# Padding the last keys of v, copying a product in its own tile, and one clamp on another engine: a fused attention and feed-forward kernel

## The chip, the cores and the metric

The kernel runs on one core of one Trainium2 chip. Its five engines each have their own queue and run in order: TensorE (PE in the profile, its weight loads are PEld), VectorE (DVE), ScalarE (ACT), GpSimd (POOL) and SyncE (SP, which only issues DMAs). The metric is the device time of one execution in microseconds, and the comparison is with the kernel before on the same chip.

## The reference

Attention over 8 batches, 8 heads, 576 tokens and 64 elements per head, in which a score that lies more than tau below its row's maximum is dropped, followed by two matmuls with a Mish between them:

```python
scores = scale * np.matmul(q, k.transpose(0, 1, 3, 2))
thresh = np.max(scores, axis=-1, keepdims=True) - tau
scores = np.where(scores >= thresh, scores, -1000000000.0)
attn = np.exp(scores - np.max(scores, axis=-1, keepdims=True))
attn = attn / (np.sum(attn, axis=-1, keepdims=True) + 1e-09)
attn_out = np.matmul(attn, v)                 # 8 x 8 x 576 x 64
x = attn_out.transpose(0, 2, 1, 3).reshape(4608, 512)
h = x @ w_in                                  # 512 -> 2048
sp = np.where(h > 20.0, h, np.log1p(np.exp(np.minimum(h, 20.0))))
out = (h * np.tanh(sp)) @ w_out               # 2048 -> 512
```

w_in and w_out reach the kernel as 64-bit floating-point numbers, which it has to turn into pairs of 32-bit parts itself.

## The kernel before

The work comes in **pairs** of heads: 8 batches with 4 pairs each, 32 pairs. Each pair is cut into 9 **tiles** of 128 query rows (8 tiles of one head each, alternating, and a ninth that holds the last 64 rows of both), 288 tiles in all, g = 0 to 287. A loop over g is software-pipelined. In the step for g it issues, in this order:

1. `begin(g + 1)`: the scores of the next tile on PE, into one of two PSUM tiles `s`. A tile `s` is free again when the masking (`masked`, on DVE) two tiles earlier has read it.
2. `product(g - lag)`, which puts the products of a finished half pair into the list `pieces`. It does so twice in a pair, for the first 256 query columns (r = 0, at g % 9 == 7) and for the other 320 (r = 1, at g % 9 == 3). The result y lies in one of **two** PSUM banks of the pool `psh`, which it shares with the results h of the first matmul of the feed-forward part.
3. `evacuate` of tile g - 3: ACT copies the transposed probabilities from PSUM into the tiles `hi` (first head) and `lo` (second head), 128 keys of each of 4 chunks in the partitions, and `tk`, which holds the last 64 keys of the first head in partitions 0 to 63 and those of the second head in partitions 64 to 127.
4. the entries of `pieces`: at g below SOON = 38 two a step, from then on all five, that is 5 chunks for each of two heads on PE.
5. row maximum (DVE), exponential (ACT), the reciprocal (DVE) and normalising (POOL) of the tile before.
6. the **gather** of a finished product: ACT copies y from PSUM to x. The gathers wait in the list `ready`, which is taken over into `done` before the pieces of a step are issued, so that a gather is issued in the step after its product. The gather of r = 1 also closes the pair: `split_x` puts the rounding of x (`xh` on ACT, `xl` on POOL) into `chores`, for the first half of the columns in the same step and for the second half two steps later.
7. `chores`: the rounding of the q and k parts of a later pair (a cast on ACT, a subtraction on POOL), at fixed steps of the 9.
8. `masked` of this tile on DVE, and a number of matmuls of the first feed-forward product (`h<-xh,w1h` and so on): `EVEN = (14, 14, 14, 0, 13, 14, 14, 0, 13)` of them at g % 9 = 0, 1, ..., so none in the two steps with a product, from g = 42 on.
9. the transposes of tile g - 2 on PE (`tp<-ident,p`, `t<-ident,p`).

Every engine executes its instructions in the order in which this loop writes them.

The weights w_in are decoded meanwhile by 32 jobs of 128 x 256 (the class `Decode`, from g = 0 on, the last ones past g = 42): `first` on ACT, then `clamp` in one step, `shift` and `join` in the next on DVE, `add` on POOL, then the upper part on ACT and the lower part on POOL or, for nine of them, on DVE. Before `clamp` in a step stands the normalising of the tile before; behind it stand the chores.

In the product a chunk of 128 keys is a matmul with 128 rows and 64 columns of weights (`vf[:, a, c]`), and the head a decides which half of the partitions of y it writes. The last 64 keys (c = 4) are a matmul with 64 rows and 64 columns for each head: `vf[rows, a, 4]` against `tail[rows, 0, :n]`, where rows are 0 to 63 for the first and 64 to 127 for the second head. In the profile these are the groups `y<-hi,vf`, `y<-lo,vf` and `y<-tk,vf`. After the attention loop come the last feed-forward products, the decoding of w_out and the second matmul (from 960 us on), which the change does not touch.

The methods and functions that the change touches:

Of the kernel before, what the change touches and what calls it, by code (L numbers as in the profile page):

```python
# [9 lines left out]
ALU = mybir.AluOpType  # L10
# [4 lines left out]
P = 128  # L15
B, H, S, D = 8, 8, 576, 64
NP = H // 2
# [11 lines left out]
VP = 32  # L29
SOON = 9 * FULL + 2  # L30
# [47 lines left out]
TOP_MAX = 122879.9921875 * 2.0**-112  # L78


def fv(ap):
    return ap.bitcast(F32)
# [36 lines left out]
class Decode:  # L119
# [16 lines left out]
        nc.scalar.activation(c, low, AF.Copy, scale=2.0**-29)  # L136

    def clamp(self):
        self.nc.vector.tensor_scalar(fv(self.b), fv(self.a), TOP_MAX, -TOP_MAX, ALU.min, ALU.max)

    def shift(self):
        self.nc.vector.tensor_scalar(self.a, self.b, 3, 0x7FFFFFF8, ALU.logical_shift_left, ALU.bitwise_and)
# [18 lines left out]
def attention_moe(tc, q, k, v, tau, w_in, w_out, out):  # L161
    nc = tc.nc
    from contextlib import ExitStack

    with ExitStack() as outer:
# [104 lines left out]
        nc = Engines(tc)  # L270
        with ExitStack() as first:
# [6 lines left out]
            with ExitStack() as att:  # L278
# [160 lines left out]
                def transposes(g):  # L439

                    both = tiles[g]["both"]
                    at = odd(g) * (S + D)
                    tp = pst.tile([P, 4, P], F32, name="tp")
                    for c in range(4):
                        nc.tensor.transpose(tp[:, c, :], both[:, at + c * P:at + (c + 1) * P], ident)
                    t5 = None
                    last = g < 9 * VP and g % 9 == 8
                    if odd(g) or last:
                        t5 = pst.tile([P, P], F32, name="t5")
                        if last:  # L450
                            nc.tensor.transpose(t5, both[:, S - P:S], ident)
                            nc.tensor.transpose(t5[:D], both[:, S - D:S], ident)
                        else:
                            nc.tensor.transpose(t5, both[:, 4 * P:5 * P], ident)
                    return tp, t5
# [51 lines left out]
                def values_full(r, pt, vf, x):  # L507
                    main, tail = pt[r][:2], pt.pop(r)[2]
                    n = (2 + r) * P - r * D
                    y = psh.tile([P, 512], F32, name="y", tag="ph")  # L510

                    def chunk(c):
                        for a in range(2):
                            rows = slice(a * D, (a + 1) * D)
                            if c < 4:
                                w, m = vf[:, a, c], main[a][:, c, :n]
                            else:
                                w, m = vf[rows, a, 4], tail[rows, 0, :n]
                            nc.tensor.matmul(y[rows, :n], w, m, start=c == 0, stop=c == 4)

                    def gather():
                        nc.scalar.copy(x[:, r * QT:r * QT + n], y[:, :n])

                    return [lambda c=c: chunk(c) for c in range(5)], gather
# [118 lines left out]
                ready = []  # L643
# [45 lines left out]
                for g in range(NT + 5):  # L689
# [15 lines left out]
                            tail_hi(g - 3)  # L705
                    if ahead:
                        tiles[g - 2]["tp"] = transposes(g - 2)
                    done = list(ready)
                    ready.clear()
                    for _ in range(5 if g >= SOON else PIECES):  # L710
                        if pieces:
                            work, then = pieces.pop(0)
                            work()
                            if then:
                                ready.append(then)
                    if g < NT:
                        tiles[g]["st"], tiles[g]["e"] = row_max(tiles[g]["s"])
                    if 1 <= g <= NT:
# [160 lines left out]
        for n in range(NG):  # L879
            c, j = divmod(n, NJ)  # L880
# [11 lines left out]
            if c == 0:  # L892
# [5 lines left out]
                for e, d in order:  # L898
                    cols = slice(2 * e * QT + d * P, 2 * e * QT + (d + 1) * P)
                    toks = slice(2 * e * QT, 2 * (e + 1) * QT)  # L900
                    for i, (x, y) in enumerate(((wh, gh), (wh, gl), (wlo, gh))):
                        nc.tensor.matmul(
                            banks[d], x[:, cols], y[:, toks],
                            start=j == e == i == 0, stop=j == NJ - 1 and e == 1 and i == 2,
# [11 lines left out]
            for k, (wi, gi) in enumerate(PRODUCTS):  # L916
                o = banks[k].rearrange("p (n t) -> p n t", t=QT)
                w, at = (wa[j], (0, 2, 3)[wi]) if wi < 3 else (ws[j], wi - 3)
                for b in range(2):
                    cols = slice(at * QT + b * P, at * QT + (b + 1) * P)  # L920
                    for i, (x, y) in enumerate(((0, 0), (0, 1), (1, 0))):
                        nc.tensor.matmul(
                            o[:, b], w[x][:, cols], gs[n][y][:, gi],
                            start=j == b == i == 0, stop=j == NJ - 1 and b == 1 and i == 2,
# [6 lines left out]
def _layout(q, k, v, tau, moe_w_in, moe_w_out):  # L931
    import numpy as np

    f = np.float32
    qt = np.asarray(q, f).reshape(B, NP, 2, S, D).transpose(0, 1, 2, 4, 3)
    qp = np.zeros((B, NP, 2, D, 1280), f)
    qp[:, :, :, :, 0:S] = qt[:, :, 0, None]
    qp[:, :, :, :, 704:768] = qt[:, :, 1, None, :, 512:]
    qp[:, :, :, :, 768:1280] = qt[:, :, 1, None, :, :512]
    kt = np.asarray(k, f).reshape(B, NP, 2, S, D).transpose(0, 1, 4, 2, 3)  # L940
    kp = np.empty((B, NP, 2, D, 2, S + D), f)
    kp[..., :D] = kt[:, :, None, :, :, S - D:]
    kp[..., D:] = kt[:, :, None]
    vt = np.asarray(v, f).reshape(B, NP, 2, S, D)
    vp = np.empty((B, NP, P, 2, 5, D), f)
    vp[:, :, :, :, :4] = vt[:, :, :, :512].reshape(B, NP, 2, 4, P, D).transpose(0, 1, 4, 2, 3, 5)
    for a in range(2):
        vp[:, :, a * D:(a + 1) * D, :, 4] = vt[:, :, :, 512:].transpose(0, 1, 3, 2, 4)
    return {
        "q": qp.reshape(B * NP, P, 1280),  # L950
        "k": kp.reshape(B * NP, P, 2, S + D),
        "v": vp.reshape(B * NP, P, 2, 5, D),
        "tau": np.full((P, 1), tau, f),
        "w_in": np.ascontiguousarray(moe_w_in).view(np.int64),
        "w_out": np.ascontiguousarray(moe_w_out).view(np.int64),
    }
# [18 lines left out]
```

## Time and profile before

| | |
|---|---|
| median of 3 runs | 1377.79 us (1375.15 to 1378.16) |
| profiled execution, whole | 1377.15 us |
| its span, first to last instruction | 1375.4 us |
| PE busy | 1318.8 us, 96% of the span |
| DVE / ACT / POOL busy | 878.1 / 848.0 / 736.9 us |
| first matmul of the feed-forward part | 130.6 us |
| last product of the attention | 949.7 us |

A row of the timeline gives the start (us), the duration (us), the engine, the source line, the operation, its output and inputs, their shapes, how many instructions were merged into the row, and in brackets the idle time of the engine before it with what ended it. All work goes through a helper, so that its line is L95. A row of a group gives the count, then the busy time (us) and the mean of one (ns), then the idle time just before them. A PE matmul's duration reaches over the start of the next one; where it is the pace that matters, starts are to be compared.

### The profile page before, as it was taken

The numbers are of one execution on the slowest core, as the hardware profiler recorded it, in microseconds if no ns is written. First come the engines' busy times: TensorE is split into PE (matmuls) and PEld (weight loads), VectorE is DVE, ScalarE is ACT, GpSimd is POOL, SyncE is SP. The second block draws the span as 40 slices with busy tenths as digits, with TensorE's granted clock in tenths as the row PEclk, the third lists the DMA queues.
The fourth block names the chain that finished last, engine by engine and source line by source line (L and its number), as shares of the span: only waits on it lengthen the run. The fifth ranks groups of instructions, "written<-read, shape, count | busy, mean of one in ns | idle before, by whom it ended". The sixth has DMA issues, their size and how long they took to land. (4 is left out here: it accounts for less than half of the span.)

```text
span 1375.4 us, 28492 instructions
## 1 busy us (share of the span) xinstructions
PE 1318.8 (96%) x9941; PEld 1164.4 (85%) x9941; DVE 878.1 (64%) x2404; ACT 848.0 (62%) x1676; POOL 736.9 (54%) x1061
## 2 busy tenths in 40 slices
PE   8888999999999999999999999999999999999998
PEld 5445888888888888888888888887978999999998
DVE  6998855555555555555555555553997666666664
ACT  4777766666666666666666666664565465555552
POOL 3789866666566656566656566642413334443331
PEclk9889999999999999999999999999999999999999
DMA  5334543323333333333333333311854444444440
GB/s 173 101 101 121 167 123 111 102 85 104 88 95 108 102 88 101 88 98 105 102 91 98 88 100 103 93 43 45 267 165 152 128 124 133 138 136 129 139 135 32
DMA packets 151904, 154.82 MB, mean 113 GB/s; under 512 B 35537, under 2 KB 128721, under 8 KB 151761
## 3 DMA queue, kind: packets, MB, share of 16 engines
q1 hardware_dynamic: 151760, 153.00, 37.0%
q8 instruction: 79, 1.29, 0.4%
q14 instruction: 65, 0.52, 0.1%
HBM read 105.78 MB, written 47.19 MB: 111 GB/s over the span
## 5 line engine op out<-in xcount | busy, mean ns | idle before, releaser
L95 DVE SCALAR_TENSOR_TENSOR p<-s,st,e 128x576 f32<-128x576 f32 x288 | 235.3, 817 | 344.4 <-ACT e L95 344.1
L95 PE MATMUL h<-xh,w1h 128*128 128x288 f32 x1024 | 306.7, 299 | 23.3 <-ACT x L95 21.7
L95 POOL TENSOR_SCALAR p<-p,st 128x576 f32<-128x576 f32 x288 | 242.3, 841 | 131.2 <-DVE st L95 92.6
L95 PE MATMUL h<-xl,w1h 128*128 128x288 f32 x1024 | 301.9, 295 | 0.0
L95 PE MATMUL h<-xh,w1l 128*128 128x288 f32 x1024 | 301.9, 295 | 0.0
L95 PE MATMUL s<-k,q 128*128 128x288 f32 (+1 forms) x1280 | 242.3, 335 | 20.1 <-DVE p L95 19.0
L95 POOL TENSOR_TENSOR z<-z 128x256 f32<-128x256 f32 x128 | 124.3, 975 | 223.1 <-DVE z L95 214.3
L95 ACT ACTIVATE e<-s,st 128x576 f32<-128x576 f32 x288 | 216.0, 750 | 26.8 <-DVE st L95 23.8
L95 PEld LDWEIGHTS h<-xh,w1h 128*128 128x128 f32 x1024 | 192.1, 188 | 31.5 <-ACT x L95 28.3
L95 DVE TENSOR_REDUCE st<-s 128x1 f32<-128x576 f32 x288 | 216.6, 752 | 2.0 <-PE s L95 1.5
L95 DVE TENSOR_TENSOR gl<-z,gh 128x1792 fp32r<-128x1792 f32 (+1 forms) x72 | 141.3, 1964 | 108.4 <-ACT gh L95 108.4
L95 ACT CAST gh<-z 128x1792 fp32r<-128x1792 f32 (+1 forms) x72 | 116.5, 1620 | 150.5 <-issue 81.2
L95 PEld LDWEIGHTS s<-k,q 128*128 128x128 f32 (+1 forms) x1280 | 171.0, 191 | 36.8 <-DVE p L95 28.7
L95 PEld LDWEIGHTS h<-xh,w1l 128*128 128x128 f32 x1024 | 192.2, 188 | 0.0
L95 PEld LDWEIGHTS h<-xl,w1h 128*128 128x128 f32 x1024 | 192.2, 188 | 0.0
L95 PE MATMUL tp<-ident,p 128*128 128x128 f32 x1152 | 179.3, 278 | 3.0 <-POOL p L95 1.2
L95 ACT COPY lo<-tp 128x512 f32<-128x512 f32 (+1 forms) x160 | 87.1, 545 | 151.5 <-PE tp L95 150.4
L95 PEld LDWEIGHTS tp<-ident,p 128*128 128x128 f32 x1152 | 135.4, 141 | 43.4 <-issue 31.0
L95 ACT COPY hi<-tp 128x512 f32<-128x512 f32 (+1 forms) x160 | 87.1, 545 | 100.5 <-PE tp L95 100.4
L95 PE MATMUL y<-hi,vf 128*64 128x320 f32 (+1 forms) x512 | 144.6, 424 | 1.0 <-ACT hst L95 1.0
L95 PE MATMUL y<-lo,vf 128*64 128x320 f32 (+1 forms) x512 | 144.5, 424 | 0.0
L95 PE MATMUL o<-gh,sl 128*128 128x256 f32 x512 | 144.5, 282 | 0.0
(67 smaller groups left out, 2774.8 us busy)
## 6 DMA issues: line engine op xcount, KB each, us to landing
z<-hd SPq DMA_DIRECT2D x144, 256.0 KB, 3.1
r<-q SPq DMA_DIRECT2D x112, 160.0 KB, 2.2
r<-k SPq DMA_DIRECT2D x112, 160.0 KB, 2.4
vf<-v SPq DMA_DIRECT2D x64, 160.0 KB, 2.7
out_t<-c SPq DMA_DIRECT2D x36, 256.0 KB, 2.4
dec<-w_in SPq DMA_DIRECT2D x32, 256.0 KB, 3.2
hd<-hst SPq DMA_DIRECT2D x16, 512.0 KB, 3.3
w<-w_out SPq DMA_DIRECT2D x16, 512.0 KB, 5.0
```

The costliest lines, as they stand in the source:

```text
L95: made = method(*args, **kwargs)
```

## The change

Three things are edited.

**Weights of the last 64 keys.** `_layout` stores them for each head in that head's half of the 128 partitions and zeros in the other half, and the matmul for c = 4 uses all 128 rows of `tail` and of the weights, like the other chunks. Before, both heads' rows stood in both columns' places and each matmul read one half. (`VP` is 32, the number of pairs, so that the line with `vp[VP:` touches nothing.)

**Result copied in the tile of its product.** From step SOON = 38 on a gather goes to `done` of the same step, so that it is issued, with the close of the pair and the first rounding of x, in the step of its product. Before step 38 it stays one step later.

**Clamp.** `Decode.clamp` is issued on GpSimd.

```diff
@@ class Decode
     def clamp(self):
-        self.nc.vector.tensor_scalar(fv(self.b), fv(self.a), TOP_MAX, -TOP_MAX, ALU.min, ALU.max)
+        self.nc.gpsimd.tensor_scalar(fv(self.b), fv(self.a), TOP_MAX, -TOP_MAX, ALU.min, ALU.max)
@@ values_full
                     def chunk(c):
                         for a in range(2):
                             rows = slice(a * D, (a + 1) * D)
-                            if c < 4:
-                                w, m = vf[:, a, c], main[a][:, c, :n]
-                            else:
-                                w, m = vf[rows, a, 4], tail[rows, 0, :n]
-                            nc.tensor.matmul(y[rows, :n], w, m, start=c == 0, stop=c == 4)
+                            m = main[a][:, c, :n] if c < 4 else tail[:, 0, :n]
+                            nc.tensor.matmul(y[rows, :n], vf[:, a, c], m, start=c == 0, stop=c == 4)
@@ the loop over g
-                    done = list(ready)
-                    ready.clear()
+                    done = ready
+                    ready = []
                     for _ in range(5 if g >= SOON else PIECES):
                         if pieces:
                             work, then = pieces.pop(0)
                             work()
                             if then:
-                                ready.append(then)
+                                (done if g >= SOON else ready).append(then)
@@ _layout
-    vt = np.asarray(v, f).reshape(B, NP, 2, S, D)
-    vp = np.empty((B, NP, P, 2, 5, D), f)
-    vp[:, :, :, :, :4] = vt[:, :, :, :512].reshape(B, NP, 2, 4, P, D).transpose(0, 1, 4, 2, 3, 5)
+    vt = np.asarray(v, f).reshape(B * NP, 2, S, D)
+    vp = np.zeros((B * NP, P, 2, 5, D), f)
+    vp[..., :4, :] = vt[:, :, :512].reshape(B * NP, 2, 4, P, D).transpose(0, 3, 1, 2, 4)
     for a in range(2):
-        vp[:, :, a * D:(a + 1) * D, :, 4] = vt[:, :, :, 512:].transpose(0, 1, 3, 2, 4)
+        vp[:, a * D:(a + 1) * D, a, 4] = vt[:, a, 512:]
+        vp[VP:, (1 - a) * D:(2 - a) * D, a, 4] = vt[VP:, a, 512:]
```

**What moves on ACT.** Here is a step with g % 9 == 3 and the step behind it, in the middle of the attention: `x<-y` is the gather of r = 1, `q` and `k` are the chores, `xh` is the rounding of x, `lo` and `tk` begin the next step, `e` is the exponential. Before:

```order
L95 ACTIVATE e<-s,st 128x576
L95 CAST q_3960<-r 128x320
L95 CAST k_3958<-r 128x320
L95 COPY lo<-tp 128x4x128
L95 COPY tk<-t_4203 128x128
L95 ACTIVATE e<-s,st 128x576
L95 COPY x<-y 128x320
L95 CAST xh<-x 128x288
L95 COPY hst<-h 128x288
```

and with the change:

```order
L95 ACTIVATE e<-s,st 128x576
L95 COPY x<-y 128x320
L95 CAST q_3961<-r 128x320
L95 CAST k_3959<-r 128x320
L95 CAST xh<-x 128x288
L95 COPY lo<-tp 128x4x128
L95 COPY tk<-t_4210 128x128
L95 ACTIVATE e<-s,st 128x576
L95 COPY hst<-h 128x288
```

The gather and the rounding of x have moved ahead of the next step's evacuation and exponential, and the two casts now stand behind the gather.

**What moves on POOL.** This is the decoding of w_in near its start; `p<-p,st` is the normalising, `dec<-dec` as TENSOR_TENSOR is `add`, `w1l` is the lower part. Before:

```order
L95 TENSOR_SCALAR p<-p,st 128x576
L95 TENSOR_TENSOR w1l<-dec,w1h 128x256
L95 TENSOR_TENSOR dec<-dec 128x256
L95 TENSOR_SCALAR st<-st 128x1
L95 TENSOR_SCALAR p<-p,st 128x576
```

and with the change:

```order
L95 TENSOR_SCALAR p<-p,st 128x576
L95 TENSOR_SCALAR dec<-dec 128x256
L95 TENSOR_TENSOR w1l<-dec,w1h 128x256
L95 TENSOR_TENSOR dec<-dec 128x256
L95 TENSOR_SCALAR st<-st 128x1
L95 TENSOR_SCALAR p<-p,st 128x576
```

The clamp, `dec<-dec` as TENSOR_SCALAR, stands behind the normalising; 32 such rows are added on POOL and 32 are gone from DVE. PE's instructions stand in the same order as before.

More of the change, by code (lines that the diff above doesn't have):

```diff
@@ L951, in _layout @@
         "k": kp.reshape(B * NP, P, 2, S + D),
-        "v": vp.reshape(B * NP, P, 2, 5, D),
+        "v": vp,
         "tau": np.full((P, 1), tau, f),
```

## The prediction, made before the change was timed

> **What bounds the kernel now.** I read the page's busy times first, then the windows by stage, then the waits, and last the timeline of one pair.
>
> ```profile
> PE 1318.8 (96%) x9941; PEld 1164.4 (85%) x9941; DVE 878.1 (64%) x2404; ACT 848.0 (62%) x1676; POOL 736.9 (54%) x1061
> ...
> 34.00:138.00 104.00, 85.36 (x490) 47.45 (x491) 95.93 (x321) 79.15 (x199) 88.16 (x131) 0.87 0.35 108
> 138.00:900.00 762.00, 741.27 (x5634) 650.35 (x5633) 446.23 (x1646) 499.38 (x1185) 471.76 (x740) 1.00 0.35 102
> ```
>
> The windows' columns are the length, then busy time on PE, PEld, DVE, ACT and POOL, the granted clock and the DMAs. PE is the bound on the average, but not everywhere. From 34 to 138 us, where w_in is decoded, DVE has 95.9 of 104 us and POOL 88.2, while PE idles. From 138 to 900 us PE has 741.3 of 762 us. The remaining 20.7 us have one name:
>
> ```profile
> PEld h L95 <- ACT x L95: 28.3, 28, 1.6
> PE h L95 <- ACT x L95: 21.7, 28, 1.4
> ...
> PEld s L95 <- DVE p L95: 0.7, 3, 0.3
> PE h L95 <- ACT x L95: 20.6, 26, 1.4
> ```
>
> The first two rows are of the whole span, the last two of 138 to 900 us. The first feed-forward matmul of a bank waits 28 times, once for each pair from the fifth on, until ACT has copied y to x and so freed its bank; the scores hardly ever wait for the masking there. One such place on PE, with r = 1:
>
> ```profile
> 505.95 0.43 PE L95 MATMUL y<-hi,vf 128*64 128x320 f32 x1
> ...
> 506.32 0.76 PE L95 MATMUL y<-tk,vf 64*64 64x320 f32 x4
> ...
> 507.00 0.66 PE L95 MATMUL tp<-ident,p 128*128 128x128 f32 x4
> ...
> 508.27 0.29 PE L95 MATMUL h<-xl,w1h 128*128 128x288 f32 x1
> 508.40 0.30 PE L95 MATMUL h<-xh,w1l 128*128 128x288 f32 x1
> 509.46 0.40 PE L95 MATMUL h<-xh,w1h 128*128 128x288 f32 x1 [0.76 <-ACT x L95]
> ...
> 511.24 0.38 PE L95 MATMUL s<-k,q 128*128 128x288 f32 x1
> ```
>
> Feed-forward matmuls start 0.13 us apart (508.27 to 508.40), here 1.06: each wait costs PE about 0.93 us. And ACT at that place:
>
> ```profile
> 504.74 0.45 ACT L95 CAST q<-r 128x320 fp32r<-128x320 f32 x1
> 505.08 0.46 ACT L95 CAST k<-r 128x320 fp32r<-128x320 f32 x1
> 507.69 0.59 ACT L95 COPY lo<-tp 128x512 f32<-128x512 f32 x1 [2.15 <-PE tp L95]
> 508.18 0.27 ACT L95 COPY tk<-t 128x128 f32<-128x128 f32 x1
> 508.33 0.76 ACT L95 ACTIVATE e<-s,st 128x576 f32<-128x576 f32 x1
> 508.97 0.44 ACT L95 COPY x<-y 128x320 f32<-128x320 f32 x1
> ...
> 509.12 0.82 DVE L95 SCALAR_TENSOR_TENSOR p<-s,st,e 128x576 f32<-128x576 f32 x1 [2.38 <-ACT e L95]
> ```
>
> ACT sat idle for 2.15 us while y was being computed; y was complete at 507.08 (506.32 + 0.76), and its copy began at 508.97, because `lo`, `tk` and the exponential stand ahead of it.
>
> **The tail of the product.** The two matmuls and their passes stay, with the same columns; only the rows grow from 64 to 128. What can change is the pace around them.
>
> ```profile
> 97.85 0.43 PE L95 MATMUL y<-hi,vf 128*64 128x320 f32 x1
> ...
> 98.12 0.43 PE L95 MATMUL y<-hi,vf 128*64 128x320 f32 x1
> 98.49 0.51 PE L95 MATMUL s<-k,q 64*128 64x288 f32 x2
> ...
> 490.14 0.38 PE L95 MATMUL y<-hi,vf 128*64 128x256 f32 x1
> ...
> 490.36 0.38 PE L95 MATMUL y<-hi,vf 128*64 128x256 f32 x1
> ...
> 490.67 0.65 PE L95 MATMUL y<-tk,vf 64*64 64x256 f32 x4
> 491.25 0.66 PE L95 MATMUL tp<-ident,p 128*128 128x128 f32 x4
> ```
>
> Matmuls of one shape follow each other every 0.27 us with 320 columns (97.85 to 98.12) and every 0.22 with 256 (490.14 to 490.36); the two heads run side by side. Where the shape changes the step is 0.37 (98.12 to 98.49, and 505.95 to 506.32) and 0.31 (490.36 to 490.67): 0.10 us more. From the tail to the transposes it is 0.68, which is two steps of 0.27 and 0.14, and 0.58, two of 0.22 and 0.14. With one shape throughout the first extra of 0.10 goes, and the second becomes that of main chunk to other shape, 0.10 in place of 0.14: 0.14 us a product. 56 products lie where PE is the bound (28 pairs, two each): **-7.8 us**. The ends: nothing, if the extra belongs to the change of weights and not of shape, and 0.24 each, 13.4 us, if both go. I take the middle, because between two other shapes (98.12 to 98.49) the extra is the same 0.10.
>
> **The gather.** Removed is the wait of 0.93 us, 28 times, 26 us. What is late next is the exponential. From the end of y, with the tail 0.10 earlier at 506.98: ACT starts 0.03 after PE's end (`lo` at 507.69 after `tp`, 507.00 + 0.66), so x begins at 507.01; then q, k and xh, each 0.34 behind the last (504.74 to 505.08); `lo` at 508.37, `tk` 0.49 and the exponential 0.64 behind it (507.69, 508.18, 508.33), at 509.01 where it was 508.33; the masking 0.79 later (508.33 to 509.12), at 509.80. The scores that need the masked tile's bank follow the start of the masking by 0.88:
>
> ```profile
> 126.35 0.82 DVE L95 SCALAR_TENSOR_TENSOR p<-s,st,e 128x576 f32<-128x576 f32 x1 [3.84 <-ACT e L95]
> ...
> 127.23 0.53 PE L95 MATMUL s<-k,q 128*128 128x288 f32 x2 [0.95 <-DVE p L95]
> ```
>
> So they can begin at 510.68. PE without any wait would be there at 511.24 - 0.14 - 0.93 = 510.17. A new wait of 0.51 us for the masking takes the place of the 0.93 for x, and 0.42 remains: 28 x 0.42 = **-11.8 us**. The ends: nothing (the chain through ACT 0.42 longer than worked out) and 26 us (0.5 shorter). At r = 0 nothing waited for x, and ACT has only x and one cast ahead of `lo`, 0.68 us behind the end of y at 491.32 (490.67 + 0.65), while `lo` needs the transposes' end at 491.91 (491.25 + 0.66) anyway: no cost.
>
> Queued behind the waiting copy are also the casts of q and k, and so POOL: their subtractions start at about 507.8 in place of 505.3, and with that of xl they hold the normalising back.
>
> ```profile
> 505.32 0.86 POOL L95 TENSOR_TENSOR q<-r,q 64x320 fp32r<-64x320 f32 x1
> ...
> L95 POOL TENSOR_TENSOR k<-r,k 128x320 fp32r<-128x320 f32 x112 | 97.7, 872 | 55.5 <-ACT k L95 53.3
> ...
> 507.41 0.82 POOL L95 TENSOR_SCALAR p<-p,st 128x576 f32<-128x576 f32 x1
> ```
>
> Three at 0.87 end at 510.4, the normalising ends about 511.5 instead of 508.2. Its transposes stand two steps on, behind the scores of 511.24 and another 14 matmuls, after 513: hidden by some 1.5 us. The moved step issues no DMA; a load that needs the buffers of q and k comes four tiles later. The close of the pair feeds the feed-forward product of the next batch two tiles later: hidden.
>
> **The clamp.** Rows of 34 to 138 us:
>
> ```profile
> L95 DVE TENSOR_SCALAR dec<-dec 128x256 f32<-128x256 f32 x24 | 10.1, 421 | 0.0
> ...
> L95 POOL TENSOR_SCALAR p<-p,st 128x576 f32<-128x576 f32 x35 | 32.5, 928 | 8.1 <-DVE st L95 2.9 <-DVE dec L95 2.9
> L95 POOL TENSOR_SCALAR st<-st 128x1 f32<-128x1 f32 x35 | 9.6, 274 | 0.0
> ```
>
> 24 clamps leave DVE, 10.1 us: it has 85.8 of 104 us then. On POOL the same kind of operation takes 274 ns for one element and 928 for 576, so 0.56 us for 256; 24 of them are 13.5 us, and POOL has 101.7 of 104. The gain can't pass 2.3 us, where POOL alone then stands; the loss is 13.5 us if every clamp lengthens POOL's queue and its idle time stays. One full engine is exchanged for another at nearly the same height: I take **0**. The 8 other clamps lie before 34 us or behind 138 us, where PE is the bound.
>
> The Trainium skill, "GPSIMD Engine Reference", in its introduction, calls GpSimd the wrong choice for ordinary elementwise work, at which VectorE is about twice as fast. By that a clamp would be 0.84 us (an estimate: twice the 421 ns), POOL would need 108 us of the 104, and the sum would be some 4 us worse; nothing above rests on it.
>
> **The sum** against the profiled execution of 1377.15 us: 1377.15 - 7.8 - 11.8 + 0 = 1357.5. That execution is 0.6 us below the median shown, so 1358 for a median; I say **1357**.
>
> **Rivals.**
>
> A. The chain through ACT doesn't bind, and the whole wait comes back: 1377.15 - 7.8 - 26 = 1343. For it: DVE and ACT are each near 60% busy from 138 to 900 us, and the casts may overlap more. Against it: four ACT instructions now stand between y and the evacuation.
>
> B. POOL becomes the bound of the decoding: DVE's `shift` waits for a clamp behind the normalising, and both idle in turn. With some 8 us of the 13.5 it gives 1357.5 + 8 = 1365. For it: 101.7 of 104 us. Against: POOL's present idle time is partly a wait for DVE, which gets faster.
>
> C. The padded tail saves nothing, since the extra belongs to the weights' change: 1357.5 + 7.8 = 1365. The Trainium skill, "TensorEngine Tiling (Array Packing)", section "Key Properties", says that a change of tiling mode drains the engine. By that rule C falls, and the trace's 0.10 us at each change of shape agrees.
>
> D. Slower: the exponential doesn't recover. One masking follows the last at the earliest through row maximum, scaling and exponential, 2.78 us:
>
> ```profile
> 486.33 0.82 DVE L95 SCALAR_TENSOR_TENSOR p<-s,st,e 128x576 f32<-128x576 f32 x1 [1.11 <-ACT e L95]
> ...
> 489.11 0.82 DVE L95 SCALAR_TENSOR_TENSOR p<-s,st,e 128x576 f32<-128x576 f32 x1 [0.91 <-ACT e L95]
> ```
>
> PE's step with 14 feed-forward matmuls is 14 x 0.13 and a tile's scores and transposes (507.00 to 508.27 less one step, 1.1), 2.9 us: nothing is made up there, so a lag of 0.5 us at one tile returns at the next ones, where casts of x and k stand on ACT too. The gather breaks even at 0.42 us a pair beyond the sum, and the whole change at 0.42 + 7.8/28 = 0.70. With 1.0 it gives 1357.5 + 28 = 1385. Against it: twice a pair PE's step holds a whole product, in which the loop catches up, and the scores' wait for the masking is now 0.7 us in 762.
>
> **How the numbers follow.** Forecast 0.55, A 0.18, B 0.10, C 0.08, D 0.09. The forecast's own range is 1350 to 1364. The range of 1343 to 1371 holds it, B and C, and half of A; it leaves out D and the rest of A. A measurement of this kernel tells about 0.2%, 2.8 us, from no change. Faster by more than that are the forecast, A, B and nearly all of C: 0.89. Within it lie D with a small lag and C together with B, 0.04; slower is the rest of D, 0.07.
>
> **What would show it.** The tail: rows `y<-tk,vf` of 128 rows that follow the last main chunk after 0.27 and 0.22 us. The gather: `PE h <- ACT x` gone from the waits, x copied straight behind y, and in its place a wait of the scores for the masking `p`, about 0.5 us, 28 times; if that row stays near zero, A holds, and if it comes several times a pair, D. The clamp: DVE's busy time from 34 to 138 us near 86 and POOL's near 102, the first feed-forward matmul still near 130 us; several us later is B. I am wrong if the scores wait for the masking longer than h waited for x, or if the decoding's end moves by more than the products gain.

## The result and the profile after

The changed kernel takes **1360.75 us** (median, 1360.31 to 1361.14) against 1377.97 for the kernel before: a ratio of 0.9875 with a 95% interval of 0.9855 to 0.9895, 17.2 us faster. The forecast was 1357, in a range of 1343 to 1371.

The page's busy times and the windows by stage of the changed kernel, with the columns as before:

```profile
PE 1311.3 (96%) x9941; PEld 1171.1 (86%) x9941; DVE 872.4 (64%) x2372; ACT 849.5 (63%) x1676; POOL 742.3 (55%) x1093
...
34.00:138.00 104.00, 83.70 (x466) 47.20 (x467) 89.44 (x289) 76.94 (x193) 91.70 (x149) 0.85 0.34 103
138.00:900.00 762.00, 750.70 (x5760) 669.38 (x5757) 454.48 (x1676) 509.46 (x1204) 477.99 (x760) 1.00 0.36 103
```

From 138 to 900 us PE is busy for 750.7 us in place of 741.3. From 34 to 138 us it does less than before (466 matmuls against 490) though DVE has become emptier. The waits of the whole span, with the engine that waits, the one waited for, the total, the count and the longest:

```profile
ACT x L95 <- PE y L95: 125.7, 57, 4.4
...
PEld s L95 <- DVE p L95: 48.9, 60, 2.4
...
PE s L95 <- DVE p L95: 31.3, 50, 2.1
```

`PE h <- ACT x`, 21.7 us before, is gone. ACT now stands idle ahead of the gather instead (125.7 us), which costs nothing by itself, and the scores wait for the masking for 31.3 us where it was 19.0.

Where the time came from is seen best at fixed points: the start of a product's tail on PE. The first four rows are of the kernel before (pair 3, r = 1; pair 5, r = 1; pair 8 and pair 28, r = 0):

```profile
123.37 0.65 PE L95 MATMUL y<-tk,vf 64*64 64x320 f32 x2
...
182.62 0.49 PE L95 MATMUL y<-tk,vf 64*64 64x320 f32 x2
...
255.28 0.65 PE L95 MATMUL y<-tk,vf 64*64 64x256 f32 x4
...
843.89 0.65 PE L95 MATMUL y<-tk,vf 64*64 64x256 f32 x4
```

and the same of the changed kernel:

```profile
124.84 0.70 PE L95 MATMUL y<-tk,vf 128*64 128x320 f32 x4
...
188.69 0.71 PE L95 MATMUL y<-tk,vf 128*64 128x320 f32 x4
...
259.32 0.60 PE L95 MATMUL y<-tk,vf 128*64 128x256 f32 x4
...
832.98 0.60 PE L95 MATMUL y<-tk,vf 128*64 128x256 f32 x4
```

At 182.62 us the changed kernel is 6.07 us **behind**, most of it lost from 123 us on. Then it gains steadily: 20 pairs take 573.66 us in place of 588.61, 0.75 us less a pair. So the change is a loss of some 6 us in the decoding of w_in and a gain of 0.75 us for each of 28 pairs behind it. (The first 100 us are no fixed points: with the same order of PE's instructions there the first product comes up to 2.5 us later than in the kernel before, in tail and gather below.)

One product with r = 1 on PE, ACT and DVE, in the changed kernel:

```profile
503.96 0.43 PE L95 MATMUL y<-hi,vf 128*64 128x320 f32 x1
...
504.23 0.71 PE L95 MATMUL y<-tk,vf 128*64 128x320 f32 x4
504.87 0.66 PE L95 MATMUL tp<-ident,p 128*128 128x128 f32 x4
...
507.73 0.60 PE L95 MATMUL tp<-ident,p 128*128 128x128 f32 x4
508.67 0.81 PE L95 MATMUL s<-k,q 128*128 128x288 f32 x4 [0.35 <-DVE p L95]
```

```profile
504.98 0.43 ACT L95 COPY x<-y 128x320 f32<-128x320 f32 x1 [2.13 <-PE y L95]
505.31 0.46 ACT L95 CAST q<-r 128x320 fp32r<-128x320 f32 x1
505.67 0.46 ACT L95 CAST k<-r 128x320 fp32r<-128x320 f32 x1
506.03 0.43 ACT L95 CAST xh<-x 128x288 fp32r<-128x288 f32 x1
506.36 0.59 ACT L95 COPY lo<-tp 128x512 f32<-128x512 f32 x1
506.84 0.27 ACT L95 COPY tk<-t 128x128 f32<-128x128 f32 x1
507.00 0.76 ACT L95 ACTIVATE e<-s,st 128x576 f32<-128x576 f32 x1
...
507.79 0.82 DVE L95 SCALAR_TENSOR_TENSOR p<-s,st,e 128x576 f32<-128x576 f32 x1 [3.03 <-ACT e L95]
```

The tail follows the last main chunk after 0.27 us and the transposes follow the tail after 0.64, 2 x 0.27 and 0.10. The gather begins 0.04 us behind the end of y (504.23 + 0.71), and four ACT instructions stand ahead of `lo`. The masking comes at 507.79 and releases the scores 0.88 us later, though PE had begun the transposes ahead of them at 507.73. From the tail to those scores it is 4.44 us; before it was 4.92 (506.32 to 511.24).

### The profile page after: what moved, and what is told of

Read it like the earlier page. It is cut to its first block, busy times and chain, and to the rows that moved or that the text cites. A ratio compares the mean times of both kernels' runs of the same rounds, so it can differ in the third digit from the quotient of the medians.

```text
span 1358.9 us, 28431 instructions
## 1 busy us (share of the span) xinstructions
PE 1311.3 (96%) x9941; PEld 1171.1 (86%) x9941; DVE 872.4 (64%) x2372; ACT 849.5 (63%) x1676; POOL 742.3 (55%) x1093
## 5 line engine op out<-in xcount | busy, mean ns | idle before, releaser
L95 PE MATMUL h<-xh,w1h 128*128 128x288 f32 x1024 | 302.6, 295 | 1.1 <-ACT hst L95 1.1
L95 PE MATMUL s<-k,q 128*128 128x288 f32 (+1 forms) x1280 | 244.3, 337 | 32.4 <-DVE p L95 31.3
L95 POOL TENSOR_TENSOR k<-r,k 128x320 fp32r<-128x320 f32 x112 | 97.9, 874 | 95.8 <-ACT k L95 93.6
L95 PE MATMUL o<-gl,sh 128*128 128x256 f32 x512 | 143.8, 281 | 0.0
```

The costliest lines, as they stand in the source:

```text
L95: made = method(*args, **kwargs)
```

## The experiments

Every kernel was timed against the kernel before. The table collects what the sections below use: the ratio with its interval, how much a pair takes less than before (from the tails of pairs 8 and 28), and how far the tail of pair 5, r = 1, falls behind (+) that of the kernel before, at 182.62 us. The last two are of one profiled execution each, and single executions differ: those of the kernel before lie between 1375.15 and 1380.71 us, and the profiled one of gather and clamp, 1370.16 us, was the slowest of its five. So 1 or 2 us in the last column tell nothing.

| kernel | median, us | ratio to before, 95% | per pair, us | at pair 5, us |
|---|---|---|---|---|
| the change | 1360.75 | 0.9875 (0.9855 to 0.9895) | -0.75 | +6.07 |
| tail alone | 1369.54 | 0.9928 (0.9914 to 0.9942) | -0.29 | -0.16 |
| gather alone | 1362.76 | 0.9880 (0.9867 to 0.9894) | -0.47 | +1.39 |
| clamp alone | 1379.72 | 1.0004 (0.9995 to 1.0012) | 0.00 | +2.17 |
| tail and gather | 1355.09 | 0.9825 (0.9811 to 0.9838) | -0.75 | -0.49 |
| tail and clamp | 1371.15 | 0.9949 (0.9935 to 0.9962) | -0.28 | +1.55 |
| gather and clamp | 1367.53 | 0.9917 (0.9904 to 0.9931) | -0.46 | +7.96 |
| casts first | 1339.76 | 0.9719 (0.9705 to 0.9732) | -1.34 | -2.08 |
| casts first, clamp | 1345.51 | 0.9762 (0.9748 to 0.9775) | -1.34 | +6.69 |
| casts first, first 15 clamps | 1338.76 | 0.9717 (0.9704 to 0.9730) | -1.34 | -1.38 |
| casts first, last 17 clamps | 1347.04 | 0.9764 (0.9751 to 0.9778) | -1.34 | +7.02 |
| the change, later shift | 1357.76 | 0.9852 (0.9839 to 0.9866) | -0.75 | +2.14 |
| casts first, clamp, later shift | 1342.03 | 0.9734 (0.9716 to 0.9752) | -1.34 | +5.70 |

### The parts one by one

The edits of these runs are those of the change's diff, each part taken or left; only the padded layout of v is in all of them, and without the tail's part the matmuls read the halves that they read before. The theory to be tested was that the parts add up, with the loss of 6 us in the clamp; its rival, that the early loss belongs to the gather, which blocks ACT while the decoding still runs.

**The tail alone.**

> The kernel before with the padded tail alone (the gather one step later and the clamp on DVE as before; v in the padded layout). Theory 1, the parts add up: each of the 64 products starts its tail 0.27 or 0.22 us behind the last main chunk in place of 0.37 or 0.31 and the transposes follow 0.04 us earlier, 0.14 us for each of the 56 products where PE is the bound, so 7.8 us faster than before. Theory 2, the extra belongs to the change of weights and not to the shape: no change.

Measured: 9.3 us faster by the medians (1378.88 to 1369.54), 0.29 us a pair, so 0.14 a product, as worked out from the two extras of 0.10 and 0.04. The extra belongs to the change of shape: the weights change just as before, and it is gone. The Trainium skill, "TensorEngine Tiling (Array Packing)", section "Key Properties", says that a change of tiling mode drains the engine; the trace agrees, with 0.10 us for each change that went.

**The gather alone.**

> The kernel before with the gather in the step of its product alone. Theory 1, the parts add up: the wait of h for x (21.7 us on PE) is gone, the scores wait for the masking about 28 times by 0.4 to 0.5 us in its place, and the pair gets about 0.45 to 0.6 us shorter: 12 to 17 us faster than before, with the products up to 190 us at the times of before. Theory 2, the late start of the changed kernel (6.1 us at 190 us) comes from the gather, which blocks ACT in the first steps from g = 38 on, where the decoding still runs: then these 6 us are here too and the gain is 6 to 11 us.

Measured: 16.1 us faster. A pair takes 0.47 us less, and the wait that takes the place of the old one is there, 27 times from 138 to 900 us:

```profile
PE s L95 <- DVE p L95: 9.2, 27, 0.4
```

At pair 5 this kernel is 1.4 us behind, not 6: the early loss isn't the gather's alone.

**The clamp alone.**

> The kernel before with the clamp on GpSimd alone. Theory 1: the 6.1 us that the changed kernel is behind at 190 us come from the clamp: DVE's shift now starts only when POOL has done the clamp and stands then against POOL's queue of long instructions (one shift took 2.42 us where 0.27 is usual), so this kernel is about 6 us slower than before. Theory 2: the late start comes from the gather, and this kernel is within 1.5 us of before.

Measured: 0.04% slower, with an interval that reaches across no change. Neither theory holds as it was written: alone, the clamp costs nothing that can be measured (theory 2's time), and the gather alone loses little either (not theory 2's cause). At pair 5 its profiled execution is 2.2 us behind, no more than single executions differ.

**Tail and gather.**

> The changed kernel with the clamp back on DVE. Theory 1: the clamp costs 6 us, so 1354 to 1355 us, 22 to 23 us below the kernel before, and the products up to 190 us come at about the times of before. Theory 2: the clamp costs nothing and the late start stays, 1360 to 1361 us.

Measured: 1355.09 us, as theory 1 said: with the clamp back on DVE the changed kernel is 5.7 us faster, and at pair 5 it is level with the kernel before. So the clamp costs some 6 us beside the other two parts and nothing that shows alone. The parts do not add up, and which of the two makes the clamp dear was the next question.

**Tail and clamp; gather and clamp.**

> The changed kernel with the gather one step later, as before. The clamp has cost 0.8 us alone, 5.7 beside tail and gather and 5.8 beside tail, gather and casts first. Theory 1, the gather makes the clamp dear (it takes away the wait of h for x that hid it): about 1 us slower than the tail alone, 1370 to 1371. Theory 2, the padded tail does, because it shifts the tiles against the decoding: 5 to 6 us slower than the tail alone, 1374 to 1376.

> The changed kernel with the unpadded tail. Theory 1, the gather makes the clamp dear: 5 to 6 us slower than the gather alone, 1368 to 1369. Theory 2, the padded tail does: 1 us slower than the gather alone, 1363 to 1364.

Measured by the ratios, the clamp adds 0.0021 to the tail (2.9 us, with an uncertainty of about 2.6) and 0.0037 to the gather (5.1 us, uncertainty 2.7); beside both it was 0.0050 (6.9 us). By these times alone the two can't be told from each other; against the clamp by itself (0.0004) only the cost beside the gather is clear of the uncertainty. The place is the same in all of them. From pair 3 to pair 5, 123 to 183 us, the profiled executions lose 2.0 us to the clamp alone and 0.7 beside the tail, but 4.8 beside the gather and 4.9 beside both. With the rows of the next section that makes the gather the likely reason; it is not settled by the times.

### What the clamp does there

In that stretch of the changed kernel stands the longest row of `shift` (DVE, TENSOR_SCALAR on uint32), which usually takes 0.27 us. DVE, then POOL, then PE:

```profile
165.03 2.42 DVE L95 TENSOR_SCALAR dec<-dec 128x256 uint32<-128x256 uint32 x1 [0.88 <-POOL dec L95]
167.37 0.81 DVE L95 SCALAR_TENSOR_TENSOR p<-s,st,e 128x576 f32<-128x576 f32 x1
...
164.59 0.41 POOL L95 TENSOR_SCALAR dec<-dec 128x256 f32<-128x256 f32 x1
164.95 0.82 POOL L95 TENSOR_TENSOR xl<-x,xh 128x288 fp32r<-128x288 f32 x1
165.73 0.87 POOL L95 TENSOR_TENSOR k<-r,k 128x320 fp32r<-128x320 f32 x1
166.55 0.73 POOL L95 TENSOR_TENSOR w1l<-dec,w1h 128x256 fp32r<-128x256 f32 x1
167.24 0.29 POOL L95 TENSOR_SCALAR st<-st 128x1 f32<-128x1 f32 x1
...
168.24 1.05 PE L95 MATMUL s<-k,q 128*128 128x288 f32 x5 [2.00 <-DVE p L95]
```

`shift` waits 0.88 us for the end of the clamp. At that moment POOL starts its next instruction, and `shift` doesn't end before POOL's row of long instructions has ended, 2.42 us later. The masking stands behind it on DVE, and PE waits 2.0 us for the masking. All 12 other shifts of this kernel that took over 0.6 us began within 0.25 us of the start of a POOL instruction and ended within 0.2 us of its end. The Trainium skill, "GPSIMD Engine Reference", section "Specifications", says that the two engines share GpSimd's SBUF interfaces and contend for them when a VectorE instruction runs in a two-port mode or reads two inputs; the rows fit it, though no run here shows in which mode `shift` runs.

The clamp's end often puts `shift` into that place. In this kernel 14 shifts began within 0.1 us of the end of their clamp. Seven of them took 0.89 us and more: a long POOL instruction had started just before. The other seven took 0.29 us: POOL's next instruction was a short one or came after `shift`, as here, DVE and then POOL:

```profile
89.05 0.29 DVE L95 TENSOR_SCALAR dec<-dec 128x256 uint32<-128x256 uint32 x1 [0.37 <-POOL dec L95]
...
89.10 0.96 POOL L95 TENSOR_TENSOR q<-r,q 64x320 fp32r<-64x320 f32 x1
```

The other six of the 13 long shifts were not released by their clamp and met a POOL instruction all the same; each cost under 0.6 us.

The gather lengthens that row of POOL instructions: it closes the pair one step earlier, so that the second `xl` falls into the step with the subtraction of k. With the gather and the late clamps on GpSimd the longest shift is 2.39 to 2.42 us in all four kernels that have the shift in its old place; with the clamp but not the gather, behind k and w1l alone, it is 1.73 and 1.70.

The next runs moved `shift` and `join` of each decoding job, and with them what follows in the job, one step later, in the changed kernel and in one that is described below:

```diff
-STAGES = ((0, 1, 1), (0, 1, 1))
+STAGES = ((0, 2, 2), (0, 2, 2))
```

> The changed kernel with shift and join of a decoding job one step later, so that DVE's shift is no longer released by the end of its clamp. Theory 1, the clamp costs because shift is released exactly when POOL starts its next long instruction and is held until POOL pauses: now shift starts behind the reciprocal, no row DVE dec waits for POOL dec, no shift takes over 1 us, and the kernel gains 3 to 6 us, 1355 to 1358. Theory 2, POOL's added work itself is the cost: 1360 to 1362 us.

> Casts first with all clamps on GpSimd, and shift and join one step later, so that no shift is released by its clamp. Theory 1, the release into POOL's next instruction is the cost: no shift over 1 us, and 1340 to 1341.5, as with the clamp on DVE. Theory 2, it is half of it, as in the changed kernel, where the later shift gave 3.0 us: 1342 to 1343.5. Theory 3, POOL's work itself is the cost: 1345 to 1346.

No DVE decoding row waits for POOL any more, and the longest shift is 0.93 and 0.92 us. The changed kernel gains 3.0 us by the medians; the intervals of the two ratios overlap at their ends (0.9839 to 0.9866 and 0.9855 to 0.9895), so it is likely rather than settled; 3.0 is the low end of what theory 1 of that run expected. The other kernel gains 0.0028 of the ratio, 3.9 us with an uncertainty of 3.1, and its median lies where theory 2 put it: about half of the clamp's cost went with the release into POOL's queue, and by the uncertainty it may be nearly nothing or nearly all. The single executions spread widely there (1339.86 to 1345.42 us for the second kernel).

The move also has a price of its own. In the profiled executions PE's transposes wait for POOL for 4.9 and 5.9 us in the two kernels, where it was 2.6 and 2.1 with the shift in its old place. So what is left of the clamp's cost is at least in part POOL's queue by another way; how it divides stays open. The same move with the clamp on DVE, which would show what the later step does by itself, was not run.

### The wait that the gather left

In the step of a product the casts of q and k could be done while y is computed, since ACT is idle then (2.13 us at 504.98 above). This edit issues them ahead of the gather, with the clamp on DVE:

```diff
+                    for work in chores.pop(g, []):
+                        work()
                     for gather, closed in done:
                         gather()
                         if closed is not None:
                             close_pair(g - XSPLIT[1], closed)
...
                     for work in chores.pop(g, []):
                         work()
```

> Tail and gather with the clamp on DVE, and in the step of a product the casts of q and k are issued ahead of the gather, so that they fill ACT's idle time while y is computed. Theory 1, the chain from the end of y through x, q, k, xh, lo, tk and the exponential sets the scores' new wait: it gets two casts, 0.7 us, shorter, the 28 waits of 0.4 us for the masking go, and the kernel comes to 1343 to 1345 us, 10 to 12 below tail and gather. Theory 2, the loop of row maximum, exponential and masking is itself as long as PE's step there: the wait only moves to a later tile, and less than 3 us is gained.

Measured: 1339.76 us, 0.9719 of the kernel before (0.9705 to 0.9732), 15.3 us below tail and gather, where theory 1 expected 10 to 12. A pair gains another 0.60 us, to 1.34, and from 138 to 900 us PE is never idle:

```profile
138.00:900.00 762.00, 761.93 (x5911) 685.99 (x5910) 465.84 (x1723) 524.97 (x1231) 484.92 (x766) 1.00 0.36 103
```

On ACT at one such place:

```profile
488.03 0.45 ACT L95 CAST q<-r 128x320 fp32r<-128x320 f32 x1
488.38 0.46 ACT L95 CAST k<-r 128x320 fp32r<-128x320 f32 x1
490.27 0.43 ACT L95 COPY x<-y 128x320 f32<-128x320 f32 x1 [1.43 <-PE y L95]
490.73 0.43 ACT L95 CAST xh<-x 128x288 fp32r<-128x288 f32 x1
491.07 0.58 ACT L95 COPY lo<-tp 128x512 f32<-128x512 f32 x1
```

From the gather to `lo` it is 0.80 us in place of 1.38, and from 138 us on the scores' wait for the masking is gone. On PE there, the tail and those scores:

```profile
489.51 0.71 PE L95 MATMUL y<-tk,vf 128*64 128x320 f32 x4
...
493.37 0.80 PE L95 MATMUL s<-k,q 128*128 128x288 f32 x4
```

That is 3.86 us without a wait, where the change has 4.44. Counted by starts the wait had cost 0.58 us, and not the 0.35 of its row, which begins only at the modelled end of the matmul before; that is why theory 1 expected too little. So the chain through ACT was the bound, and not the masking's loop. This kernel beats both the kernel before and the change.

The same with the clamp on GpSimd, for all jobs, for the first 15 and for the last 17 (`work.early = n < 15`, or `n >= 15`, picks the engine in `clamp`):

> The same with the clamp on GpSimd. Theory 1, the clamp costs 6 us beside the gather but under 1 us without it because the gather holds back the casts, and so POOL's subtractions, its next normalising and the clamp: with the casts ahead again, the clamp costs 1 to 2 us. Theory 2, the clamp's cost is a collision of DVE's shift with whatever POOL runs behind the clamp, and how much of it reaches PE depends on the times at which the tiles fall: it costs 3 to 6 us here too.

> The same with the clamp on GpSimd for the first 15 of the 32 decoding jobs only, whose clamps lie ahead of the first q and k subtractions on POOL. Theory 1, DVE is the bound there and POOL has room: 1 to 3 us faster than with all clamps on DVE (the kernel with the clamp alone was 1.3 to 2.7 us ahead of before up to 100 us). Theory 2, the gain is lost again in the steps after: no change.

> Casts first with the clamp on GpSimd for the last 17 of the 32 decoding jobs only, the complement of the run with the first 15. Theory 1, the clamp costs where POOL also has the subtractions of q, k and xl: the whole 5.8 us are here, 1344.5 to 1346. Theory 2, the cost is spread over all clamps and the early ones only chanced to be free: 1341 to 1343.

All clamps on GpSimd cost 0.0043 of the ratio, 5.9 us, here too, although the gather no longer holds back the casts. That is what theory 2 of that run said, and the explanation by the casts falls. The first 15 clamps gain nothing that can be told (0.9717 against 0.9719), and the last 17 cost the whole (0.9764). The cost lies with the later jobs, in whose steps POOL also has the subtractions of q, k and xl, and the room that DVE gets in the first 100 us is of no use. That these subtractions are the reason rests on the rows at 165 us, and not on this run alone.

## Why the prediction was right, and where it was not

**The tail** held: -7.8 us for 56 products, 0.14 each, was 0.143 each in the trace. The rival that the extra belongs to the weights (C) is gone.

**The gather** held in its mechanism and nearly in its size. The chain was worked out as 4.46 us from the tail to the scores (506.22 to 510.68) and was 4.44 (504.23 to 508.67). The new wait for the masking is there, 28 times, and 0.47 us a pair came back where 0.42 was expected. Both waits were larger than worked out: the old one cost about 1.05 us a pair and not 0.93 (casts first, where PE waits for neither, gains 1.34, of which 0.29 are the tail's), the new one 0.58 and not 0.51. The end of the attention gained about 2 us more that the sum didn't hold. They come with the gather (the gather alone gains 1.8 us behind its last product, the tail alone nothing); that the last pair closes a step earlier too is the likely reason, which no run singles out. Rival A, that the chain doesn't bind, was wrong for the change, and casts first shows what it would have been worth: 15 us. Rival D didn't come: behind 200 us the change has the wait once a pair, 0.4 us at most by its rows, and with casts first PE never waits for the masking there.

**The clamp** was the step that failed, inside its bounds: taken at 0, it cost 6 us beside the other parts. "One full engine is exchanged for another at nearly the same height" was wrong in both halves. In the window of 34 to 138 us of the changed kernel:

```profile
L95 POOL TENSOR_SCALAR dec<-dec 128x256 f32<-128x256 f32 x22 | 8.8, 398 | 0.0
...
L95 DVE TENSOR_SCALAR dec<-dec 128x256 uint32<-128x256 uint32 x22 | 11.8, 535 | 2.9 <-POOL dec L95 2.9
```

A clamp on POOL takes 0.40 us, not 0.56 (nor the 0.84 of the estimate beside it), and POOL isn't full, 91.7 us and not 101.7; DVE kept 89.4 us and not 85.8, since `shift`, 0.36 us before, now takes 0.54. What the sum of busy times couldn't hold is the order: a DVE instruction that waits for POOL in the middle of DVE's queue, and that meets POOL's next instruction when it is released. Rival B had that wait, and 1365 for its price; it came with 6 of its 8 us, though not because POOL was full. The sign named for it came too, faintly: the first feed-forward matmul begins at 133.2 us where it was 130.7.

So the products gained some 3 us more than forecast, about two thirds of that at the attention's end, the clamp lost 6, and 1360.75 stands 3.75 us above 1357. That it is so near is partly luck, since the two misses have opposite signs.

## What to carry to other kernels

When a wait is taken away, follow the instructions that move ahead of others on the engine that did the work: here four ACT instructions between a product and the next exponential gave back over half of the gain (0.58 of 1.05 us a pair), and doing two of them in the idle time ahead of the product brought it all. An instruction moved to another engine with room there can still cost, if the engine that it left now waits for it in the middle of its queue. And parts that are free alone should be timed together: the clamp cost nothing that could be measured by itself and some 6 us beside the gather and the tail.

## What was not expected of the hardware

A VectorE instruction of 0.27 us took up to 2.42 us while GpSimd ran several instructions back to back, and ended only when their row did. Released 0.05 us ahead of such an instruction it took 0.29 us. So the moment of its release counts: with the same clamps on GpSimd and `shift` one step later, the longest took 0.93 us.

The granted clock of PE in the first stage isn't the same in the profiled executions of two kernels, though PE's instructions stand in the same order there. The window of 34 to 69 us of the kernel before:

```profile
34.00:69.00 35.00, 29.28 (x155) 14.98 (x157) 32.51 (x116) 25.99 (x67) 27.45 (x43) 0.81 0.31 100
```

and of tail and gather:

```profile
34.00:69.00 35.00, 27.27 (x176) 14.31 (x176) 32.96 (x114) 26.80 (x69) 28.27 (x43) 1.00 0.32 100
```

0.81 in the one and 1.00 in the other; DVE is the busiest engine there in both, with 32.5 and 33.0 of 35 us, and at pair 5 the two are within 0.5 us of each other. With one profile of each kernel it isn't shown whether the clock goes with the kernel or with the execution.
